# Fourier mixing and a squared-ReLU feed-forward layer on one core: a reordered prologue, half-width sine tables, weights staged in f32, and batch folds spaced out

## The chip, the cores and the metric

The kernel runs on one core of a Trainium2 chip. The metric is the device time of one execution in microseconds; a kernel is run several times and the median is quoted. The profiled span is a little shorter than the device time of the same execution (693.4 against 695.2 us for the kernel before). Engines are named as in the profile: PE (matmul), PEld (its weight loads), DVE (vector), ACT (scalar), POOL (which here issues most of the loads) and SP (which issues the stores). All runs in this text were in the fast state, and all of them gave correct results.

## The reference, cut to what matters

```python
def _attn_ref(x):                       # x: 8 x 3008 x 256, f32
    X = np.fft.fft(x, axis=1)
    X = np.fft.fft(X, axis=2)
    return X.real.astype(np.float32)

def _moe_ref(x, w_in, w_out):           # x: 24064 x 256, w_in: 256 x 2048, w_out: 2048 x 256
    h = np.maximum(x @ w_in, 0.0)
    return (h * h @ w_out).astype(np.float32)
```

## The kernel before: the parts that matter

The two transforms become matmuls with cosine and sine tables. Symmetry lets the kernel fold each batch first (sums and differences of mirrored rows and columns: `u`, `v`, `w` on DVE) and then multiply by tables a quarter as long. The transform over the 256 features is merged into w_in (`gmat` makes G1, G2 and G3). What is left per batch is a small block of table matmuls (`stage1_ops`, PSUM tile `pf`) in two blocks (even and odd frequencies), and then the long pipeline in steps of 256 columns and 256 hidden features.

```python
def gmat(c):                            # merged weights, 512 columns at a time
    ...                                 # 4 matmuls from cosD, sinD and win16
    act(G1[:, cs], pc, AF.Copy, bias=0.0, scale=1.0 / HS)
    act(G2[:, cs], ps, AF.Copy, bias=0.0, scale=-1.0 / HS)
    ts(out=G3[:, cs], in0=ps, scalar1=s3[:, 0:1], scalar2=None, op0=ALU.mult)

def fold_ops(b):                        # a list of 24 entries per batch: DVE operations and one load
    ...
    ops = [pair(q) for q in range(NQ)] + [pair0]      # x4 -> u, 6 x 0.68 us
    if b + 1 < B:
        ops.append(lambda: load_x(b + 1))             # x4 is free: start the next load
    ...                                               # u -> v -> w

alloc_pq(0)
fe, fo = fold_ops(0)
for f in table_ops(0) + fe: f()         # sine tables of block 0, then batch 0's fold
for c in range(F // 512): gmat(c)
for f in stage1_ops(0, 0, True): f()
...
spread(fo, 1, 5)                        # side work, laid into the steps
spread(table_ops(1), 4, 10)             # the tables of block 1
spread(stage1_ops(0, 1, True), 10, 16)
FOLD = {0: [1, 2, 3], 1: [4], 2: [5], 3: [6, 7]}      # during batch 0: fold 1, 2 and 3
...
for si, (c, fp) in enumerate(steps):    # 384 steps
    cur = x_front(c, fp)                # matmuls with G1, G2; first ReLU on ACT
    if prev is not None: x_back(prev)   # matmuls with G3; second ReLU; two squares on DVE
    ...                                 # 8 output matmuls (po) of an earlier chunk
    for f in side.get(si, []): f()
```

There is one buffer for x (`x4`), 24 KB on each partition. In the first eight steps there are no output matmuls, so PE has only 0.64 us of work a step there.

Of the kernel before, what the change touches and what calls it, by code (L numbers as in the profile page):

```python
# [9 lines left out]
F32 = mybir.dt.float32  # L10
F16 = mybir.dt.float16
I32 = mybir.dt.int32
AF = mybir.ActivationFunctionType
# [4 lines left out]
HS = 32.0  # L18
# [4 lines left out]
def kernel(  # L23
# [32 lines left out]
    bfp = ctx.enter_context(tc.tile_pool(name="bfp", bufs=4))  # L56
# [3 lines left out]
    tgp = ctx.enter_context(tc.tile_pool(name="tgp", bufs=2))  # L60
# [31 lines left out]
    zt = const.tile([4 * NQ, D], F32, name="zt")  # L92
    nc.vector.memset(zt, 0.0)
# [16 lines left out]
    def load_mid(b, eng):  # L110
        eng.dma_start(out=xm[:, 1 : NQ + 2 : NQ], in_=x[b : b + 1, 0 : M + 1 : M])
        eng.dma_start(out=xm[:, 3 : 3 * NQ + 3 : 3 * NQ - 1], in_=x[b : b + 1, QN : S : M])
# [13 lines left out]
    nc.scalar.dma_start(out=xm, in_=zt)  # L126
    load_mid(0, nc.scalar)
    win16 = const.tile([P, 2, F], F16, name="win16")
    for c in range(2):
        cs = slice(c * F // 2, (c + 1) * F // 2)  # L130
        nc.gpsimd.dma_start(out=win16[:, :, cs],
                            in_=moe_w_in[:, cs].rearrange("(c p) f -> p c f", p=P))
    wout16 = const.tile([P, NFC, D], F16, name="wout16")
    nc.gpsimd.dma_start(out=wout16, in_=moe_w_out.rearrange("(c p) o -> p c o", p=P))
# [4 lines left out]
    def vec(name, w=1):  # L139
        return const.tile([P, w], F32, name=name)  # L140
# [25 lines left out]
    ts(out=s3, in0=sgn, scalar1=2.0 / HS, scalar2=None, op0=ALU.mult)  # L166
# [10 lines left out]

    cosD = const.tile([P, 2, P], F16, name="cosD")
    sinD = const.tile([P, 2, P], F16, name="sinD")
    for c in range(2):  # L180
        dv = tgp.tile([P, 1], F32, name="dv", tag="dv")
        ts(out=dv, in0=pidx, scalar1=float(c * P), scalar2=None, op0=ALU.add)
        t = tgp.tile([P, P], F32, name="td", tag="td")
        ts(out=t, in0=jrow, scalar1=dv[:, 0:1], scalar2=1.0 / D, op0=ALU.mult, op1=ALU.mult)
        ts(out=t, in0=t, scalar1=R23, scalar2=None, op0=ALU.add)
        ts(out=t, in0=t, scalar1=R23, scalar2=-float(D), op0=ALU.subtract, op1=ALU.mult)
        m = tgp.tile([P, P], F32, name="md", tag="md")
        stt(out=m, in0=jrow, scalar=dv[:, 0:1], in1=t, op0=ALU.mult, op1=ALU.add)
        stt(out=t, in0=m, scalar=-1.0, in1=m, op0=ALU.mult, op1=ALU.max)
        act(sinD[:, c, 0 : P - 1], m[:, 0 : P - 1], AF.Sin, bias=0.0, scale=wD)  # L190
        act(cosD[:, c, 0 : P - 1], t[:, 0 : P - 1], AF.Sin, bias=hpi[:, 0:1], scale=-wD)  # L191
        nc.vector.memset(cosD[:, c, P - 1 : P], 1.0)
        nc.vector.tensor_copy(sinD[:, c, P - 1 : P], alt)
# [4 lines left out]

    def table_ops(blk):
        c0, n = BLK[blk]  # L200
        cs = slice(c0, c0 + n)

        def two(q0):
            qs = (q0, q0 + 1)
            t = {q: tgp.tile([P, HE], F32, name="tt", tag="tt")[:, 0:n] for q in qs}
            m = {q: tgp.tile([P, HE], F32, name="tm", tag="tm")[:, 0:n] for q in qs}
            for q in qs:
                ts(out=t[q], in0=krow[:, cs], scalar1=nfrac[:, q : q + 1], scalar2=R23,  # L208
                   op0=ALU.mult, op1=ALU.add)
            for q in qs:  # L210
                ts(out=t[q], in0=t[q], scalar1=R23, scalar2=-float(S),  # L211
                   op0=ALU.subtract, op1=ALU.mult)
            for q in qs:
                stt(out=m[q], in0=krow[:, cs], scalar=nval[:, q : q + 1], in1=t[q],  # L214
                    op0=ALU.mult, op1=ALU.add)
                act(sinT[:, q, cs], m[q], AF.Sin, bias=0.0, scale=tsc[:, q : q + 1])  # L216
            for q in qs:
                stt(out=t[q], in0=m[q], scalar=-1.0, in1=m[q], op0=ALU.mult, op1=ALU.max)
                act(cosT[:, q, cs], t[q], AF.Sin, bias=bcos[:, q : q + 1],  # L219
                    scale=tneg[:, q : q + 1])  # L220

        return [(lambda q=q: two(q)) for q in range(0, NQ, 2)]
# [3 lines left out]
    G3 = const.tile([P, F], F16, name="G3")  # L226

    def gmat(c):
        cs = slice(c * 512, (c + 1) * 512)
        pc = psx.tile([P, 512], F32, name="pc", tag="x")  # L230
        for t in range(2):
            mm(pc, cosD[:, t, :], win16[:, t, cs], t == 0, t == 1)
        ps = psx.tile([P, 512], F32, name="ps", tag="x")
        for t in range(2):
            mm(ps, sinD[:, t, :], win16[:, t, cs], t == 0, t == 1)
        act(G1[:, cs], pc, AF.Copy, bias=0.0, scale=1.0 / HS)
        act(G2[:, cs], ps, AF.Copy, bias=0.0, scale=-1.0 / HS)
        ts(out=G3[:, cs], in0=ps, scalar1=s3[:, 0:1], scalar2=None, op0=ALU.mult)

    eall = const.tile([P, 2, NQ, B], F16, name="eall")  # L240
    ez = const.tile([P, 2, NQ, P], F16, name="ez")
    nc.vector.memset(ez, 0.0)
    bf = {}
    PQ = {}
# [3 lines left out]
    def fold_ops(b):  # L248
# [22 lines left out]
        def edges(s):  # L271
            def f():
                nc.vector.tensor_copy(w[k, s, :, P - 1], v[k, s, :, 0])
                if b == 0:
                    nc.vector.tensor_copy(ez[k, s, :, P - 1], v[k, s, :, P])
                else:
                    nc.vector.tensor_copy(eall[k, s, :, b], v[k, s, :, P])
            return f
# [199 lines left out]
    for f in table_ops(0) + fe:  # L478
        f()
    for c in range(F // 512):  # L480
        gmat(c)
    for f in stage1_ops(0, 0, True):
        f()

# [4 lines left out]
    side = {}  # L489

    def spread(ops, lo, hi):
        for i, f in enumerate(ops):
            side.setdefault(lo + int((hi - lo) * i / len(ops)), []).append(f)

    spread(fo, 1, 5)
    spread(table_ops(1), 4, 10)
    spread(stage1_ops(0, 1, True), 10, 16)
    FOLD = {0: [1, 2, 3], 1: [4], 2: [5], 3: [6, 7]}
    EGRP = {0: [1, 2, 3], 3: [4, 5, 6, 7]}
    for b in range(B - 1):  # L500
        s0 = first_step[b]
        L = first_step[b + 1] - s0
        at = lambda z: s0 + int(z * (L - 1))
        f0_, f1_ = (0.3, 0.85) if b == 0 else (0.05, 0.75)
        nf = FOLD.get(b, [])
        for i, bb in enumerate(nf):
            w_ = (f1_ - f0_) / len(nf)
            spread(sum(fold_ops(bb), []), at(f0_ + w_ * i), at(f0_ + w_ * (i + 1)))
        side.setdefault(at(0.0) + 1, []).append(lambda bb=b + 1: alloc_pq(bb))
        spread(stage1_ops(b + 1, 0) + stage1_ops(b + 1, 1), at(0.55 if b == 0 else 0.05), at(0.85))  # L510
        if b in EGRP:
            spread(e_ops(EGRP[b]), at(0.87), at(0.97))
            side.setdefault(at(0.97), []).append(lambda bb=b + 1: e_row(bb))
        else:
            side.setdefault(at(0.3), []).append(lambda bb=b + 1: e_row(bb))
# [54 lines left out]
```

## Time and profile before

| | before |
|---|---|
| device time, median of the 4 runs beside the changed kernel | 695.44 us |
| PE busy | 92% of 693.4 us |
| PE busy from 0 to 140 us | 89.5 us |
| PE's longest waits | 26.6 us for ACT's ReLU, 17.9 us for w_in |

The first look is the page: the share of each of 40 slices (17.3 us each) in tenths.

```profile
PE   0748676999999999999999999999999999999998
PEclk9978988999999999999999999999999999999999
DMA  8920755518111631153101011111011111111111
```

PE is full from the eighth slice on, so nearly all that can be saved by feeding PE lies in the first 130 us. The table of stretches says it with numbers. Columns: the stretch, its length, busy us (and instructions) of PE, PEld, DVE, ACT, POOL, then the granted clock, the DMA engines' busy share and GB/s.

```profile
10.00:20.00 10.00, 2.12 (x6) 0.72 (x6) 8.96 (x21) 6.07 (x11) 3.72 (x4) 1.00 1.04 198
40.00:50.00 10.00, 2.97 (x14) 1.75 (x13) 8.22 (x24) 4.67 (x9) 0.00 (x0) 0.64 0.00 0
50.00:60.00 10.00, 5.92 (x34) 4.09 (x34) 6.66 (x18) 7.81 (x16) 0.00 (x0) 0.68 0.01 2
80.00:90.00 10.00, 2.31 (x21) 1.83 (x19) 2.40 (x5) 0.27 (x1) 1.84 (x3) 0.86 0.55 155
200.00:400.00 200.00, 200.00 (x1927) 175.12 (x1925) 126.82 (x342) 162.32 (x288) 17.11 (x20) 1.00 0.25 72
```

PE's list of waits, whole (us in total, times, longest):

```profile
PE xb L74 <- ACT r L460: 26.6, 6, 8.6
PE pc L74 <- DMA win_128<-in_moe_w_in_dram: 17.9, 1, 17.9
PE xb L74 <- DVE qt L338: 2.3, 2, 1.6
PE pc L74 <- DVE G_200 L238: 1.8, 1, 1.8
PE ps L74 <- ACT G_198 L236: 1.5, 2, 0.8
```

"Waiting for ACT's ReLU" doesn't yet say why the ReLU is late. The chain of waits around 80 us shows one of the causes: ACT waited for DVE, and DVE waited for x. Columns: start, us, what.

```profile
79.42 0.30 issue
79.73 7.85 DMA x_110<-in_x_dram,idx
87.60 0.21 DVE u L255
```

**A measure used all through this text.** I call the end of the second ReLU of a step the end of that step. Up to step 36, PE streams 63.99 us worth of matmul columns, counted in the trace at 2.4 GHz (all matmuls that start before the end of step 36, zeros left out). The number is the same in every kernel below. So the end of step 36 less 63.99 us is the time lost by then. The clock comes from the Trainium skill ("TensorE: Matmul & The Clock Gate", first table: up to 2.4 GHz). The trace agrees: matmuls of 256 columns start 0.11 us apart when nothing holds them. In the kernel before, step 36 ends at 131.31 us, so 67.3 us are lost.

### The profile page before, as it was taken

Reading aid. Unit: us, or ns where it says so; the run is one execution under the profiler, and the core shown is the slowest. Engines: PE = TensorE matmul, PEld = TensorE weight load, DVE = VectorE, ACT = ScalarE, POOL = GpSimd, SP = SyncE. Lnnn points to the kernel's source line nnn. Section 1 sums busy time; section 2 is a strip of 40 time slices with the busy share of each in tenths; the row PEclk is TensorE's granted clock in tenths of the full one; section 3 lists DMA queues with packets and bytes.
Section 4 is the critical chain, followed back from the end, with each engine's and each line's share of the span. In section 5 each row is a group of like instructions: output and inputs, shape, how many; then the busy total and the mean of one; then the engine's idle time right before and its main releaser. Section 6 shows DMA issues by size and latency. Waiting matters only on the chain.

```text
span 693.4 us, 14967 instructions
## 1 busy us (share of the span) xinstructions
PE 639.5 (92%) x5924; PEld 551.3 (80%) x5924; DVE 414.5 (60%) x1131; ACT 521.1 (75%) x936; POOL 79.6 (11%) x89
## 2 busy tenths in 40 slices
PE   0748676999999999999999999999999999999998
PEld 0326564788889888888878888898889888998886
DVE  8777487676656666488754555555554555545442
ACT  4467454778888888878878888878888878888883
POOL 6400653303000400040000000000000000000000
PEclk9978988999999999999999999999999999999999
DMA  8920755518111631153101011111011111111111
GB/s 215 215 51 20 206 150 132 155 45 204 49 39 47 166 92 46 47 151 107 47 31 48 31 46 42 37 47 48 31 47 47 32 46 41 46 38 46 48 46 48
DMA packets 37766, 52.56 MB, mean 76 GB/s; under 512 B 5136, under 2 KB 31304, under 8 KB 37696
## 3 DMA queue, kind: packets, MB, share of 16 engines
q0 software_dynamic: 9680, 25.36, 15.4%
q1 hardware_dynamic: 27972, 26.22, 11.9%
q8 instruction: 46, 0.75, 0.5%
q14 instruction: 24, 0.20, 0.1%
q10 hardware_dynamic: 44, 0.03, 0.0%
HBM read 29.00 MB, written 24.64 MB: 77 GB/s over the span
## 4 chain that ended last, share of the span: by engine, by line
PE 84%; DVE 6%; ACT 3%; POOL 2%; DMA 2%; issue 2%; DVEq 0%; ACTq 0%
PE po L74 46%; PE xb L74 34%; PE pf L74 5%; POOL x_110 L101 2%; DVE u L255 2%; DMA x_110<-in_x_dram,idx 1%; ACT sinT L216 1%; DMA x_110<-in_x_dram 1%; ACT cosT L219 1%; ACT r L460 1%; DVE tt L211 1%; DVE tm L214 1%; DVE tt L208 0%; ACT r L470 0%; DVE h_370 L474 0%
## 5 line engine op out<-in xcount | busy, mean ns | idle before, releaser
L460 ACT ACTIVATE r<-xb 128x512 f16<-128x512 f32 (+1 forms) x384 | 226.4, 590 | 114.9 <-PE xb L74 84.6
L470 ACT ACTIVATE r<-xb 128x512 f16<-128x512 f32 (+1 forms) x384 | 226.2, 589 | 21.7 <-PE xb L74 3.2
L74 PE MATMUL xb<-qt,G_199 128*128 128x256 f16 (+8 forms) x880 | 189.1, 258 | 2.3 <-DVE qt L338 2.3
L74 PE MATMUL xb<-pt,G_198 128*128 128x256 f16 (+8 forms) x880 | 189.8, 259 | 0.4
L74 PE MATMUL xb<-qt,G_200 128*128 128x256 f16 (+8 forms) x880 | 147.3, 259 | 26.6 <-ACT r L460 26.6
L74 PEld LDWEIGHTS <-G_200 128*128 128x128 f16 x880 | 82.0, 98 | 37.0 <-issue 27.7
L74 PEld LDWEIGHTS <-G_198 128*128 128x128 f16 x880 | 84.1, 98 | 16.3 <-issue 5.7
L74 PEld LDWEIGHTS <-G_199 128*128 128x128 f16 x880 | 81.1, 98 | 17.0 <-issue 1.7
L101 POOL DMA_INDIRECT x_110<-in_x_dram,idx x48 | 59.5, 1240 | 14.5 <-issue 14.3
L404 ACT ACTIVATE os<-po 128x512 f32<-128x512 f32 (+1 forms) x95 | 56.3, 592 | 5.0 <-PE po L74 4.0
L255 DVE TENSOR_TENSOR u<-x_110 127x510 f16<-127x510 f32 x48 | 31.0, 683 | 16.8 <-DMA x_110<-in_x_dram,idx 10.3
L116 POOL DMA_DIRECT2D x_110<-in_x_dram x14 | 7.9, 566 | 217.9 <-DVE u L259 217.9
L74 PE MATMUL pf<-cosT,w 127*128 127x377 f16 (+1 forms) x96 | 30.1, 341 | 0.0
L74 PE MATMUL pf<-sinT,w 127*127 127x377 f16 (+1 forms) x96 | 29.8, 335 | 0.0
L74 PEld LDWEIGHTS <-w 127*128 127x128 f16 (+1 forms) x192 | 23.3, 122 | 3.9 <-issue 1.4
L74 PE MATMUL pc<-win_128,cosD 128*128 128x512 f16 x8 | 4.1, 614 | 19.7 <-DMA win_128<-in_moe_w_in_dram 17.9
L267 DVE TENSOR_TENSOR w<-v 127x381 f16<-127x381 f16 x64 | 20.9, 354 | 0.0
L262 DVE TENSOR_TENSOR v<-u 127x512 f16<-127x512 f16 x48 | 18.9, 418 | 0.1
L74 PEld LDWEIGHTS <-cosD 128*128 128x128 f16 x8 | 1.0, 126 | 21.7 <-ACT cosD L191 9.2
L309 ACT ACTIVATE as<-pf 128x377 f32<-128x377 f32 (+7 forms) x34 | 16.6, 487 | 1.6 <-PE pf L74 1.4
L216 ACT ACTIVATE sinT<-tm,tsc 128x377 f16<-128x377 f32 (+1 forms) x12 | 6.8, 610 | 12.2 <-DVE tm L214 12.2
L74 PE MATMUL po<-wout_131,h_738 128*128 128x256 f16 x64 | 10.5, 291 | 0.0
(264 smaller groups left out, 1179.8 us busy)
## 6 DMA issues: line engine op xcount, KB each, us to landing
out_dram<-os SPq DMA_DIRECT2D x157, 128.0 KB
x_110<-in_x_dram POOLq DMA_DIRECT2D x14, 756.0 KB
x_110<-in_x_dram SPq DMA_DIRECT2D x6, 252.0 KB
win_128<-in_moe_w_in_dram POOLq DMA_DIRECT2D x2, 512.0 KB
wout_131<-in_moe_w_out_dram POOLq DMA_DIRECT2D x1, 1024.0 KB
x_110<-in_x_dram,idx POOLq DMA_INDIRECT x48
x_110<-in_x_dram POOLq DMA_DIRECT2D x14, 2.0 KB
out_dram<-os SPq DMA_DIRECT2D x2, 108.0 KB
```

What stands on the lines that cost most here:

```text
L74: nc.tensor.matmul(o, l, r, start=start, stop=stop, skip_group_check=True)
L101: nc.gpsimd.indirect_dma_start(out=x4[0:NP, 2 + s, 2 * part : 2 * part + 2, :].rearrange("p q d -> p (q d)"), out_offset=None, in_=bass.AP ...
L116: nc.gpsimd.dma_start(out=x4[0:NP, s, :, :], in_=up(b, s, 0, NQ))
L211: ts(out=t[q], in0=t[q], scalar1=R23, scalar2=-float(S), op0=ALU.subtract, op1=ALU.mult)
L216: act(sinT[:, q, cs], m[q], AF.Sin, bias=0.0, scale=tsc[:, q : q + 1])
L255: return lambda: vt(u[k, :, q, 1:D], x4[k, 0:2, q, 1:D], x4[k, 3:1:-1, NQ - 1 - q, D - 1 : 0 : -1], op=ALU.add)
L262: return lambda: vt(v[k, s, q : q + 2, :], u[k, 0, q : q + 2, :], u[k, 1, q : q + 2, :], op=ALU.subtract if s else ALU.add)
L267: return lambda: vt(w[k, i, q : q + 3, 0 : P - 1], v[k, s, q : q + 3, 1:P], v[k, s, q : q + 3, D - 1 : P : -1], op=ALU.add if i < 2 else A ...
L309: act(st["a"][0:m, :], st[0][0:m, :], AF.Copy, bias=0.0, scale=1.0) \
L404: act(os_[0:m], st["o"][0:m], AF.Copy, bias=0.0, scale=HS * HS)
L460: act(r[:, 0, :, 0:n], xb[:, :, 0:n], AF.Relu)
L470: act(r[:, 1, :, 0:n], xb[:, :, 0:n], AF.Relu)
```

## The change

Its intent is to start PE earlier and to keep it fed in the first 130 us.

- The sine tables are computed for half of their columns; the other half is the mirror image with a sign (twelve small copies per block, on ACT for block 0, on DVE for block 1).
- The weights come in as f32, into the buffers that later hold h, and ACT and DVE cast them. Before, the DMA cast them on the way.
- Ten matmuls on zeros run on PE while it has nothing to do.
- The tables come first, then the 128x128 matrices, then the fold. Only half of the merged weights are made before step 0.
- Only batch 1 is folded during batch 0; three batches follow in batch 1, well apart. Batch 1's "E" rows (the single middle feature column) are multiplied inline, as batch 0's were.

The diff, cut to its core:

```diff
-    nc.scalar.dma_start(out=xm, in_=zt)
-    load_mid(0, nc.scalar)
+    nc.sync.dma_start(out=xm, in_=zt)
+    load_mid(0, nc.sync)
...
-    for c in range(2):                       # cast in the DMA
-        nc.gpsimd.dma_start(out=win16[:, :, cs], in_=moe_w_in[...])
-    nc.gpsimd.dma_start(out=wout16, in_=moe_w_out...)
+    wst = h2p.tile([P, 2, F], F32, name="wst", tag="h2")
+    wot = h2p.tile([P, NFC, D], F32, name="wot", tag="h2")
+    for c in range(4):
+        nc.gpsimd.dma_start(out=wst[:, :, cs], in_=moe_w_in[...])
+    nc.gpsimd.dma_start(out=wot, in_=moe_w_out...)
...
+    def gcast(c, cp): cp(win16[:, :, cs], wst[:, :, cs])
+    def wcast(c): nc.vector.tensor_copy(wout16[:, cs, :], wot[:, cs, :])
...
     def table_ops(blk):
-        cs = slice(c0, c0 + n)
+        ng = (n + 1) // 2
+        cs = slice(c0, c0 + ng)              # Sin for these columns only
+        def mir(q, on_act): ...              # dst = d[:, q, c0 + n - 1 : ... : -1]
...
-    for f in table_ops(0) + fe: f()
-    for c in range(F // 512): gmat(c)
-    for f in stage1_ops(0, 0, True): f()
+    for i in range(NQ // 2): rd0[i](); tr0[2 * i](); tr0[2 * i + 1]()
+    nc.vector.memset(ez, 0.0)
+    dmats()
+    for f in mi0: f()
+    warm = psx.tile([P, 512], F32, name="warm", tag="x")
+    for _ in range(10):
+        mm(warm, cosD[:, 1, :], ez[:, 0, 0:4, :], True, True)
+    for f in fe: f()
+    gcast(0, nc.scalar.copy); gmat(0); rd1[0]()
+    ...                                      # stage1(0, 0), gcast(1), gmat(1), gcast(2), gcast(3)
...
-    spread(fo, 1, 5)
-    spread(table_ops(1), 4, 10)
-    spread(stage1_ops(0, 1, True), 10, 16)
-    FOLD = {0: [1, 2, 3], 1: [4], 2: [5], 3: [6, 7]}
+    spread([rd1[1], rd1[2]], 0, 2)
+    spread(tr1, 1, 4)
+    spread(fo, 2, 5)
+    spread(mi1, 5, 7)
+    spread([(lambda c=c: wcast(c)) for c in range(4)], 6, 9)
+    spread(stage1_ops(0, 1, True), 9, 13)
+    FOLD = {0: [(1, 0.35, 0.52)], 1: [(2, 0.02, 0.2), (3, 0.38, 0.56), (4, 0.7, 0.85)],
+            2: [(5, 0.1, 0.4)], 3: [(6, 0.1, 0.4)], 4: [(7, 0.1, 0.4)]}
```

More of the change, by code (lines that the diff above doesn't have):

```diff
@@ L55 @@
     uvp = ctx.enter_context(tc.tile_pool(name="uvp", bufs=1))
-    bfp = ctx.enter_context(tc.tile_pool(name="bfp", bufs=4))
+    bfp = ctx.enter_context(tc.tile_pool(name="bfp", bufs=3))
     pp = ctx.enter_context(tc.tile_pool(name="pp", bufs=2))
@@ L59 @@
     asp = ctx.enter_context(tc.tile_pool(name="asp", bufs=2))
-    tgp = ctx.enter_context(tc.tile_pool(name="tgp", bufs=2))
+    tgp = ctx.enter_context(tc.tile_pool(name="tgp", bufs=1))
     rp = ctx.enter_context(tc.tile_pool(name="rp", bufs=3))
@@ L92 @@
     zt = const.tile([4 * NQ, D], F32, name="zt")
+    ez = const.tile([P, 2, NQ, P], F16, name="ez")
     nc.vector.memset(zt, 0.0)
@@ L125 @@
             gather(0, 1 - s, NQ // 2 - 1 - part)
-    nc.scalar.dma_start(out=xm, in_=zt)
-    load_mid(0, nc.scalar)
+    nc.sync.dma_start(out=xm, in_=zt)
+    load_mid(0, nc.sync)
     win16 = const.tile([P, 2, F], F16, name="win16")
-    for c in range(2):
-        cs = slice(c * F // 2, (c + 1) * F // 2)
-        nc.gpsimd.dma_start(out=win16[:, :, cs],
-                            in_=moe_w_in[:, cs].rearrange("(c p) f -> p c f", p=P))
     wout16 = const.tile([P, NFC, D], F16, name="wout16")
-    nc.gpsimd.dma_start(out=wout16, in_=moe_w_out.rearrange("(c p) o -> p c o", p=P))
+    wst = h2p.tile([P, 2, F], F32, name="wst", tag="h2")
+    wot = h2p.tile([P, NFC, D], F32, name="wot", tag="h2")
+    for c in range(4):
+        cs = slice(c * F // 4, (c + 1) * F // 4)
+        nc.gpsimd.dma_start(out=wst[:, :, cs],
+                          in_=moe_w_in[:, cs].rearrange("(c p) f -> p c f", p=P))
+    nc.gpsimd.dma_start(out=wot, in_=moe_w_out.rearrange("(c p) o -> p c o", p=P))
     wS = 2.0 * math.pi / S
@@ L165 @@
     s3 = vec("s3")
-    ts(out=s3, in0=sgn, scalar1=2.0 / HS, scalar2=None, op0=ALU.mult)
+    ts(out=s3, in0=sgn, scalar1=-2.0, scalar2=None, op0=ALU.mult)
     ts(out=sgn, in0=sgn, scalar1=2.0, scalar2=-1.0, op0=ALU.mult, op1=ALU.add)
@@ L176 @@
     ts(out=alt, in0=alt, scalar1=4.0, scalar2=None, op0=ALU.mult)
+    nalt = vec("nalt")
+    ts(out=nalt, in0=alt, scalar1=-1.0, scalar2=None, op0=ALU.mult)
+    alt1 = vec("alt1")
+    stt(out=alt1, in0=top, scalar=2.0, in1=alt, op0=ALU.mult, op1=ALU.add)
+    nalt1 = vec("nalt1")
+    ts(out=nalt1, in0=alt1, scalar1=-1.0, scalar2=None, op0=ALU.mult)
+    MIR = [(nalt, nalt), (alt1, nalt1), (alt, alt), (nalt, alt), (nalt, nalt), (alt, nalt)]
     cosD = const.tile([P, 2, P], F16, name="cosD")
@@ L179, with dmats @@
     sinD = const.tile([P, 2, P], F16, name="sinD")
-    for c in range(2):
+    def dmats():
         dv = tgp.tile([P, 1], F32, name="dv", tag="dv")
-        ts(out=dv, in0=pidx, scalar1=float(c * P), scalar2=None, op0=ALU.add)
-        t = tgp.tile([P, P], F32, name="td", tag="td")
-        ts(out=t, in0=jrow, scalar1=dv[:, 0:1], scalar2=1.0 / D, op0=ALU.mult, op1=ALU.mult)
-        ts(out=t, in0=t, scalar1=R23, scalar2=None, op0=ALU.add)
-        ts(out=t, in0=t, scalar1=R23, scalar2=-float(D), op0=ALU.subtract, op1=ALU.mult)
-        m = tgp.tile([P, P], F32, name="md", tag="md")
-        stt(out=m, in0=jrow, scalar=dv[:, 0:1], in1=t, op0=ALU.mult, op1=ALU.add)
-        stt(out=t, in0=m, scalar=-1.0, in1=m, op0=ALU.mult, op1=ALU.max)
-        act(sinD[:, c, 0 : P - 1], m[:, 0 : P - 1], AF.Sin, bias=0.0, scale=wD)
-        act(cosD[:, c, 0 : P - 1], t[:, 0 : P - 1], AF.Sin, bias=hpi[:, 0:1], scale=-wD)
-        nc.vector.memset(cosD[:, c, P - 1 : P], 1.0)
-        nc.vector.tensor_copy(sinD[:, c, P - 1 : P], alt)
+        ts(out=dv, in0=pidx, scalar1=float(P), scalar2=None, op0=ALU.add)
+        dvs = (pidx, dv)
+        t = [tgp.tile([P, P], F32, name="td", tag=f"td{_}") for _ in range(2)]
+        m = [tgp.tile([P, P], F32, name="md", tag=f"md{_}") for _ in range(2)]
+        for c in range(2):
+            ts(out=t[c], in0=jrow, scalar1=dvs[c][:, 0:1], scalar2=1.0 / D,
+               op0=ALU.mult, op1=ALU.mult)
+        for c in range(2):
+            ts(out=t[c], in0=t[c], scalar1=R23, scalar2=None, op0=ALU.add)
+        for c in range(2):
+            ts(out=t[c], in0=t[c], scalar1=R23, scalar2=-float(D), op0=ALU.subtract, op1=ALU.mult)
+        for c in range(2):
+            stt(out=m[c], in0=jrow, scalar=dvs[c][:, 0:1], in1=t[c], op0=ALU.mult, op1=ALU.add)
+        for c in range(2):
+            stt(out=t[c], in0=m[c], scalar=-1.0, in1=m[c], op0=ALU.mult, op1=ALU.max)
+            nc.vector.memset(cosD[:, c, P - 1 : P], 1.0)
+            nc.vector.tensor_copy(sinD[:, c, P - 1 : P], alt)
+            act(sinD[:, c, 0 : P - 1], m[c][:, 0 : P - 1], AF.Sin, bias=0.0, scale=wD)
+            act(cosD[:, c, 0 : P - 1], t[c][:, 0 : P - 1], AF.Sin, bias=hpi[:, 0:1], scale=-wD)
@@ L197, with red @@
     BLK = ((0, HE), (HE, HO))
+    HG = HE // 2 + 1
     def table_ops(blk):
         c0, n = BLK[blk]
-        cs = slice(c0, c0 + n)
-        def two(q0):
+        ng = (n + 1) // 2
+        cs = slice(c0, c0 + ng)
+        tb = {}
+        def red(q0):
+            if q0 == 0:
+                tb["t"] = tgp.tile([P, NQ, HG], F32, name="tt", tag="tt")
+                tb["m"] = tgp.tile([P, NQ, HG], F32, name="tm", tag="tm")
             qs = (q0, q0 + 1)
-            t = {q: tgp.tile([P, HE], F32, name="tt", tag="tt")[:, 0:n] for q in qs}
-            m = {q: tgp.tile([P, HE], F32, name="tm", tag="tm")[:, 0:n] for q in qs}
+            t, m = tb["t"][:, :, 0:ng], tb["m"][:, :, 0:ng]
@@ L207, in two @@
             for q in qs:
-                ts(out=t[q], in0=krow[:, cs], scalar1=nfrac[:, q : q + 1], scalar2=R23,
+                ts(out=t[:, q], in0=krow[:, cs], scalar1=nfrac[:, q : q + 1], scalar2=R23,
                    op0=ALU.mult, op1=ALU.add)
             for q in qs:
-                ts(out=t[q], in0=t[q], scalar1=R23, scalar2=-float(S),
+                ts(out=t[:, q], in0=t[:, q], scalar1=R23, scalar2=-float(S),
                    op0=ALU.subtract, op1=ALU.mult)
             for q in qs:
-                stt(out=m[q], in0=krow[:, cs], scalar=nval[:, q : q + 1], in1=t[q],
+                stt(out=m[:, q], in0=krow[:, cs], scalar=nval[:, q : q + 1], in1=t[:, q],
@@ L215, in two @@
                     op0=ALU.mult, op1=ALU.add)
-                act(sinT[:, q, cs], m[q], AF.Sin, bias=0.0, scale=tsc[:, q : q + 1])
             for q in qs:
-                stt(out=t[q], in0=m[q], scalar=-1.0, in1=m[q], op0=ALU.mult, op1=ALU.max)
-                act(cosT[:, q, cs], t[q], AF.Sin, bias=bcos[:, q : q + 1],
-                    scale=tneg[:, q : q + 1])
-        return [(lambda q=q: two(q)) for q in range(0, NQ, 2)]
+                stt(out=t[:, q], in0=m[:, q], scalar=-1.0, in1=m[:, q], op0=ALU.mult, op1=ALU.max)
@@ new lines, in trig, with mir @@
+        def trig(q):
+            act(sinT[:, q, cs], tb["m"][:, q, 0:ng], AF.Sin, bias=0.0, scale=tsc[:, q : q + 1])
+            act(cosT[:, q, cs], tb["t"][:, q, 0:ng], AF.Sin, bias=bcos[:, q : q + 1],
+                scale=tneg[:, q : q + 1])
+        def mir(q, on_act):
+            nm = n // 2
+            src = slice(c0, c0 + nm)
+            a, b = (cosT, sinT) if q % 2 else (sinT, cosT)
+            for d, sr, sc in ((cosT, a, MIR[q][0]), (sinT, b, MIR[q][1])):
+                dst = d[:, q, c0 + n - 1 : c0 + n - 1 - nm : -1]
+                if on_act:
+                    act(dst, sr[:, q, src], AF.Copy, bias=0.0, scale=sc[:, 0:1])
+                else:
+                    ts(out=dst, in0=sr[:, q, src], scalar1=sc[:, 0:1], scalar2=None, op0=ALU.mult)
@@ L224 @@
+        return ([(lambda q=q: red(q)) for q in range(0, NQ, 2)],
+                [(lambda q=q: trig(q)) for q in range(NQ)],
+                [(lambda q=q: mir(q, blk == 0)) for q in range(NQ)])
     G1 = const.tile([P, F], F16, name="G1")
@@ L226, with gcast @@
     G3 = const.tile([P, F], F16, name="G3")
+    def gcast(c, cp):
+        cs = slice(c * 512, (c + 1) * 512)
+        cp(win16[:, :, cs], wst[:, :, cs])
     def gmat(c):
@@ L237, in gmat, with gneg @@
         act(G2[:, cs], ps, AF.Copy, bias=0.0, scale=-1.0 / HS)
-        ts(out=G3[:, cs], in0=ps, scalar1=s3[:, 0:1], scalar2=None, op0=ALU.mult)
+    def gneg(c):
+        cs = slice(c * 512, (c + 1) * 512)
+        ts(out=G3[:, cs], in0=G2[:, cs], scalar1=s3[:, 0:1], scalar2=None, op0=ALU.mult)
     eall = const.tile([P, 2, NQ, B], F16, name="eall")
-    ez = const.tile([P, 2, NQ, P], F16, name="ez")
-    nc.vector.memset(ez, 0.0)
     bf = {}
+    INL = (0, 1)
     PQ = {}
@@ L273, in f @@
                 nc.vector.tensor_copy(w[k, s, :, P - 1], v[k, s, :, 0])
-                if b == 0:
+                if b in INL:
                     nc.vector.tensor_copy(ez[k, s, :, P - 1], v[k, s, :, P])
@@ L477 @@
     fe, fo = fold_ops(0)
-    for f in table_ops(0) + fe:
-        f()
-    for c in range(F // 512):
-        gmat(c)
-    for f in stage1_ops(0, 0, True):
-        f()
+    rd0, tr0, mi0 = table_ops(0)
+    rd1, tr1, mi1 = table_ops(1)
+    for i in range(NQ // 2):
+        rd0[i]()
+        tr0[2 * i]()
+        tr0[2 * i + 1]()
+    nc.vector.memset(ez, 0.0)
+    dmats()
+    for f in mi0:
+        f()
+    warm = psx.tile([P, 512], F32, name="warm", tag="x")
+    for _ in range(10):
+        mm(warm, cosD[:, 1, :], ez[:, 0, 0:4, :], True, True)
+    for f in fe:
+        f()
+    gcast(0, nc.scalar.copy)
+    gmat(0)
+    rd1[0]()
+    s1 = stage1_ops(0, 0, True)
+    for f in s1[0:NQ]:
+        f()
+    gcast(1, nc.vector.tensor_copy)
+    for f in s1[NQ:]:
+        f()
+    gneg(0)
+    gmat(1)
+    gneg(1)
+    for c in (2, 3):
+        gcast(c, nc.vector.tensor_copy)
     steps = [(c, fp) for c in range(len(chunks)) for fp in range(NF)]
@@ L489 @@
     side = {}
+    pre = {}
     def spread(ops, lo, hi):
@@ L493, in spread, with wcast @@
             side.setdefault(lo + int((hi - lo) * i / len(ops)), []).append(f)
-    spread(fo, 1, 5)
-    spread(table_ops(1), 4, 10)
-    spread(stage1_ops(0, 1, True), 10, 16)
-    FOLD = {0: [1, 2, 3], 1: [4], 2: [5], 3: [6, 7]}
-    EGRP = {0: [1, 2, 3], 3: [4, 5, 6, 7]}
+    for c in range(2, F // 512):
+        side.setdefault(2 * c - 4, []).extend([lambda c=c: gmat(c), lambda c=c: gneg(c)])
+    def wcast(c):
+        cs = slice(c * NFC // 4, (c + 1) * NFC // 4)
+        nc.vector.tensor_copy(wout16[:, cs, :], wot[:, cs, :])
+    spread([rd1[1], rd1[2]], 0, 2)
[6 more added lines that the diff above has]
+            2: [(5, 0.1, 0.4)], 3: [(6, 0.1, 0.4)], 4: [(7, 0.1, 0.4)]}
+    ST1 = {0: (0.55, 0.95), 1: (0.25, 0.85)}
+    EGRP = {1: [2, 3, 4], 4: [5, 6, 7]}
     for b in range(B - 1):
@@ L503 @@
         at = lambda z: s0 + int(z * (L - 1))
-        f0_, f1_ = (0.3, 0.85) if b == 0 else (0.05, 0.75)
-        nf = FOLD.get(b, [])
-        for i, bb in enumerate(nf):
-            w_ = (f1_ - f0_) / len(nf)
-            spread(sum(fold_ops(bb), []), at(f0_ + w_ * i), at(f0_ + w_ * (i + 1)))
+        for bb, lo, hi in FOLD.get(b, []):
+            spread(sum(fold_ops(bb), []), at(lo), at(hi))
         side.setdefault(at(0.0) + 1, []).append(lambda bb=b + 1: alloc_pq(bb))
-        spread(stage1_ops(b + 1, 0) + stage1_ops(b + 1, 1), at(0.55 if b == 0 else 0.05), at(0.85))
+        lo, hi = ST1.get(b, (0.05, 0.85))
+        spread(stage1_ops(b + 1, 0, b + 1 in INL) + stage1_ops(b + 1, 1, b + 1 in INL), at(lo), at(hi))
         if b in EGRP:
-            spread(e_ops(EGRP[b]), at(0.87), at(0.97))
+            spread(e_ops(EGRP[b]), at(0.87), at(0.96))
             side.setdefault(at(0.97), []).append(lambda bb=b + 1: e_row(bb))
-        else:
+        elif b + 1 not in INL:
             side.setdefault(at(0.3), []).append(lambda bb=b + 1: e_row(bb))
```

## The prediction

> What bounds the kernel now. From about 130 us to the end TensorE decides: the table of stretches has it busy 200.00 of 200 us in both long stretches, and it waits for nothing after 140 us. The cost is in the start. From 0 to 140 us PE is busy only about 89.5 us; its list of waits names 26.6 us on ACT (r, first ReLU), the longest 8.6 us, and 17.9 us on the DMA of w_in. Counting matmul columns at 2.4 GHz against the end of each ReLU step, some 65 us of the first 131 us (37 steps) are lost: 28.6 before step 0 ends at 36.6 us; about 16 in steps 4 to 9; 2 at step 15; 10 at steps 20-21; 9 at steps 28-30. Later steps lose about 0.045 us each.
>
> Who causes it. In the timeline DVE starts the batch fold (u) only at 19.9 us, though x has landed by about 14 us: the sine tables come first. At 41 to 58 us the second table block's reductions and Sin calls (0.61 and 0.69 us each) sit in order before the ReLUs. The chain of waits shows the folds of batches 2 and 3 waiting for x loads started only when the fold before freed the single x buffer: 7.9 and 5.5 us of DMA, loads of 20 and 16 us. While PE idles its granted clock falls to 0.64-0.68 (40-60 us). The Trainium skill ("TensorE: Matmul & The Clock Gate", "Why this matters for your kernels") says a few us of idleness return the clock to half; these stretches agree.
>
> The change, costed (estimates from these durations).
> 1. Half-width tables: a pair of reductions costs DVE about 1.9 instead of 3.1 us; tables, zeroing and D matrices end at about 13 us, the fold at 20 instead of 26. Twelve mirrors on ACT (2.6 to 4 us) end at 16-18 us.
> 2. f32 weights: twice the bytes landed, 4.2 MB at about 215 GB/s: w_in quarters at 17 to 25 us, w_out at 34, x of batch 1 at 48-50 instead of 39.5. The first cast on ACT, 1 us; seven on DVE, 0.6 to 1.1 us each. Batch 1 is folded at step 13 (about 50 us): tight, not late.
> 3. Ten zero matmuls fill idle PE time and keep the clock; worth 1 us at most.
> 4. Step 0 ends at about 26.5 us (-10). Steps 0 to 9 are then DVE-bound (about 18 us): step 9 at 46 instead of 60.3.
> 5. Spaced folds: loads finish before their folds; the stops at steps 15, 20-21, 28-30 (21 us) nearly vanish. Three dense folds in batch 1 may stop PE 0.5 to 1 us each.
> 6. Added PE work: batch 1's E rows inline, 12 matmuls of 377 columns, 1.9 us.
>
> Sum: 10 + 4 + 21, less 1.9 and about 2 of new stops: about 32 us, all on the critical path, as PE is saturated behind it; steady part and tail stay. Predicted 662 us, range 654 to 670. Faster by over 2%: 0.97; within 2%: 0.025; slower: 0.005.
>
> What would show it: u starts at 13-14 us; step 0's second ReLU ends at 25-28; step 9 at 44-48; no PE wait over 2 us after 50; DMA busy unbroken until about 48; PE busy share about 96%.
>
> What would make it wrong: DVE standing in order at a cast whose quarter lands late, pushing step 0 to 30 us; w_out's cast delaying the first output matmuls; batch 1's x late at step 13; batch 4's fold (step 72) meeting an unfinished load.

## The result, and the profile after

The changed kernel takes 663.78 us (median of 4, 663.04 to 664.68) against 695.44 us; the ratio is 0.9546, with a 95% interval from 0.9525 to 0.9567. Ratios in this text are the mean time of one kernel's fast runs over that of the other's fast runs of the same rounds, so not quite the ratio of the medians. Two more sets of the changed kernel gave 664.90 us (ratio 0.9563) and 663.63 us (0.9560).

The slices and the stretches after:

```profile
PE   1679999999999999999999999999999999999997
PEclk9989999999999999999999999999999999999999
DMA  7963614584528111541111111111111111111111
```

```profile
10.00:20.00 10.00, 5.46 (x17) 2.12 (x18) 9.53 (x35) 8.21 (x22) 8.21 (x10) 1.00 0.77 234
20.00:30.00 10.00, 7.37 (x43) 4.07 (x42) 8.44 (x25) 6.00 (x13) 5.27 (x5) 1.00 1.04 313
30.00:40.00 10.00, 5.23 (x30) 3.33 (x30) 8.58 (x32) 9.68 (x22) 3.17 (x3) 0.90 1.01 204
40.00:50.00 10.00, 9.11 (x70) 6.96 (x69) 9.62 (x29) 6.45 (x13) 0.00 (x0) 0.93 0.30 69
80.00:90.00 10.00, 10.00 (x88) 8.46 (x87) 5.78 (x15) 7.76 (x14) 0.00 (x0) 1.00 0.18 54
```

PE is full from 50 us on, where before it was full only from 130 us on. Its waits are now small, except the first one:

```profile
PE warm L74 <- ACT cosD L212: 13.7, 1, 13.7
PE xb L74 <- ACT r L507: 2.9, 2, 1.4
PE pc L74 <- DVE win_129 L271: 2.0, 2, 1.3
PE ps L74 <- ACT r L517: 1.9, 1, 1.9
PE po L74 <- DVE wout_130 L571: 0.9, 1, 0.9
```

The ends of steps, from the traces of one profiled execution each (us; the runs below are in the table as well):

| kernel | step 0 | step 9 | step 19 | step 20 | step 27 | step 28 | step 36 | lost by then | step 383 |
|---|---|---|---|---|---|---|---|---|---|
| before | 36.57 | 60.26 | 79.78 | 91.34 | 104.57 | 114.48 | 131.31 | 67.3 | 685.65 |
| changed | 29.14 | 46.87 | 65.28 | 66.83 | 79.21 | 81.06 | 96.19 | 32.2 | 653.49 |
| folds alone | 35.72 | 59.40 | 80.67 | 82.49 | 95.48 | 97.34 | 112.47 | 48.5 | 670.05 |
| prologue alone | 29.04 | 47.20 | 65.17 | 78.27 | 92.33 | 101.39 | 119.09 | 55.1 | 673.47 |
| before, two x buffers | 35.70 | 59.39 | 80.57 | 82.10 | 95.06 | 98.32 | 113.63 | 49.6 | 670.91 |
| changed, full tables | 34.82 | 53.77 | 72.03 | 73.58 | 85.96 | 87.82 | 102.94 | 39.0 | 660.20 |
| changed, cast in the DMA | 27.60 | 45.27 | 63.53 | 65.07 | 77.46 | 79.31 | 94.44 | 30.4 | 652.02 |
| that, late tables, fold at 16 | 26.88 | 42.31 | 60.91 | 62.86 | 75.67 | 77.52 | 92.65 | 28.7 | 650.19 |

Of the 35.1 us won by step 36, 7.4 come before step 0 ends, 6.0 between steps 0 and 9 (17.7 instead of 23.7 us), and 21.7 between steps 9 and 36 (49.3 instead of 71.1 us). After step 36, 3.0 us are given back; of these, 1.9 us are PE work that the change adds (606.1 us of columns in all against 604.2).

### The profile page after: what moved, and what is told of

It reads as the page before. It is cut to its first block, busy times and chain, and to the rows that moved or that the text cites. A ratio compares the mean times of both kernels' runs of the same rounds, so it can differ in the third digit from the quotient of the medians.

```text
span 661.3 us, 15041 instructions
## 1 busy us (share of the span) xinstructions
PE 634.9 (96%) x5946; PEld 549.9 (83%) x5946; DVE 408.8 (62%) x1152; ACT 523.3 (79%) x949; POOL 91.5 (14%) x91
## 4 chain that ended last, share of the span: by engine, by line
PE 93%; DVE 2%; ACT 2%; POOL 1%; issue 1%; DMA 1%; POOLq 0%
PE po L74 50%; PE xb L74 37%; PE pf L74 6%; POOL x_110 L102 1%; DMA x_110<-in_x_dram,idx 1%; ACT sinT L246 0%; ACT cosT L247 0%; ACT r L507 0%; ACT r L517 0%; DVE u L302 0%; DVE w L314 0%; PE pc L74 0%; DVE win_129 L271 0%; ACT G_183 L281 0%; DVE v L309 0%
## 5 line engine op out<-in xcount | busy, mean ns | idle before, releaser
L74 PEld LDWEIGHTS <-G_184 128*128 128x128 f16 x880 | 80.8, 97 | 17.1 <-issue 1.3
L102 POOL DMA_INDIRECT x_110<-in_x_dram,idx x48 | 69.7, 1452 | 20.3 <-issue 13.4
L74 PE MATMUL warm<-ez,cosD 128*128 128x512 f16 x10 | 4.2, 601 | 13.7 <-ACT cosD L212 13.7
L356 ACT ACTIVATE as<-pf 128x377 f32<-128x377 f32 (+5 forms) x32 | 15.5, 486 | 0.9 <-PE pf L74 0.8
L74 PE MATMUL po<-wout_130,h_387 128*128 128x256 f16 x64 | 9.6, 272 | 0.9 <-DVE wout_130 L571 0.9
L74 PE MATMUL po<-wout_130,h_761 128*128 128x256 f16 x64 | 9.6, 273 | 0.0
```

The source lines that it names most:

```text
L74: nc.tensor.matmul(o, l, r, start=start, stop=stop, skip_group_check=True)
L102: nc.gpsimd.indirect_dma_start(out=x4[0:NP, 2 + s, 2 * part : 2 * part + 2, :].rearrange("p q d -> p (q d)"), out_offset=None, in_=bass.AP ...
L356: act(st["a"][0:m, :], st[0][0:m, :], AF.Copy, bias=0.0, scale=1.0) \
```

## The experiments

Eleven runs: eight edited kernels, one of them twice, and the changed kernel itself twice as a yardstick. They are told by subject, not in the order in which they ran.

### The two halves of the change, each alone

The kernel before with only the new fold schedule:

```diff
 # in the kernel before
-    FOLD = {0: [1, 2, 3], 1: [4], 2: [5], 3: [6, 7]}
-    EGRP = {0: [1, 2, 3], 3: [4, 5, 6, 7]}
+    FOLD = {0: [(1, 0.35, 0.52)], 1: [(2, 0.02, 0.2), (3, 0.38, 0.56), (4, 0.7, 0.85)], ...}
+    ST1 = {0: (0.55, 0.95), 1: (0.25, 0.85)}
+    EGRP = {1: [2, 3, 4], 4: [5, 6, 7]}      # and INL = (0, 1)
```

> The kernel before, with only the new schedule of folds, second-stage blocks and E rows (batch 1's E rows inline). Theory: its stops at steps 15, 20-21 and 28-30 (about 21 us) came of the time that an x load takes into the one buffer, so they vanish although each fold is as dense as before (24 operations in 7 to 9 steps); the added inline E rows cost 1.9 us: 675 to 679 us. Rival: the stops come of the density of fold work on DVE; then they stay, moved to batch 1, and the time is 690 us or more.

Measured: 678.16 us (ratio 0.9746, interval 0.9721 to 0.9771). Steps 20 and 28 end 1.8 and 1.9 us after steps 19 and 27, where before it took 11.6 and 9.9 us. A fold still has its 24 entries in 7 to 9 steps, so the density of the folds was not what stopped PE there. (The profile is of the slowest of the four runs, 679.63 us; the fastest took 675.95 us.)

The changed kernel with the old fold schedule is the counterpart (`FOLD`, `ST1`, `EGRP` and `INL` put back, `bfp` with 4 buffers).

> The changed kernel with the schedule of folds, blocks and E rows of before (bfp again 4). Theory: the prologue alone brings 12 to 15 us and the stops of about 19 us come back around steps 20 and 28: 680 to 684 us, and the two parts add up (this gain plus that of the run with the new folds alone is the whole within 2 us). Rival: the parts depend on one another, because the earlier start lets the x loads collide with the weights or with one another; then the sum misses by over 4 us.

Measured: 683.34 us (0.9837, 0.9815 to 0.9858). The stops are back. PE's list of waits of this run begins:

```profile
PE xb L74 <- ACT r L507: 18.4, 4, 10.6
PE warm L74 <- ACT cosD L212: 14.0, 1, 14.0
```

and its chain of waits shows what lies behind the ReLU:

```profile
67.17 0.82 POOL x L102
67.98 0.18 issue
68.16 6.36 DMA x<-in_x_dram
74.52 0.01 issue
74.53 0.10 DVE u L302
```

The two gains in medians of the same rounds are 17.1 and 11.9 us, together 29.0, where the whole change brought 31.7. So they don't quite add up: I had expected a miss within 2 us or over 4 us, and it is 2.7 us (4.1 us at step 36 in the traces). The table shows where. With the early prologue and the old folds, step 20 takes 13.1 us instead of 11.6: the load takes nearly as long as before (18.8 us from issue to the fold's first use, against 19.7), but PE gets to the fold sooner (step 19 ends 9.5 us after the load's issue instead of 11.8), so it waits longer. An earlier start is thus partly eaten by the load time unless the folds are moved too. By the times alone the 2.7 us are not clear of the noise, as the runs of the folds alone spread over 3.7 us; the longer stop is what the traces show. In the run with the folds alone, a stop of 1.9 us at step 15 and one of 1.2 us at step 10 remain, which the whole change doesn't have.

### One load, one buffer: the cause of the large stops

If the stops are the time of a load into the only x buffer, a second buffer must remove them without touching the schedule:

```diff
 # in the kernel before
-    x4 = xp.tile([P, 4, NQ, D], F32, name="x4")
+    x4s = [xp.tile([P, 4, NQ, D], F32, name=f"x4{i}", tag=f"x4{i}") for i in range(2)]
...
-        if b + 1 < B:
-            ops.append(lambda: load_x(b + 1))
+        if b + 2 < B:                        # load_x(1) is issued after the weights
+            ops.append(lambda: load_x(b + 2))
...
-    osp = ctx.enter_context(tc.tile_pool(name="osp", bufs=4))
+    osp = ctx.enter_context(tc.tile_pool(name="osp", bufs=2))
```

> The kernel before with its own prologue and its own schedule of folds, but with two buffers for x, so that the load of batch b+2 starts when batch b has been folded (the output staging shrinks from 4 to 2 buffers to make room). If the stops at steps 20-21 and 28-30 are the time of a load into the one buffer, they vanish with no change of the schedule: 695 less 17 to 19 us, 675 to 680 us. If the density of the folds on DVE were the cause, the stops stay: 690 to 697 us. A slip of under 2 us from the smaller output staging would show as ACT waiting for a DMA of os.

Measured: 681.29 us (0.9806, 0.9786 to 0.9825), 13.5 us less than before, so somewhat less than I had expected; the stop at step 20 is gone (1.5 us), and that at step 28 as well (3.3 us, of which 3.1 are matmul columns). Its list of waits has kept the waits of the first steps and gained one:

```profile
PE xb L74 <- ACT r L463: 13.0, 5, 5.8
PE xb L74 <- DMA qt<-es: 1.3, 1, 1.3
```

At step 36 it stands at 113.6 us, 17.7 us ahead of before, as much as I had expected of the stops; 3 us of that are lost later, 1.4 of them at step 39, where PE waits for the E row of batch 1, which the faster steps reach before its copy has landed. Spacing the folds and a second buffer cure the same stop, each in its own way. Since this run left the folds as dense and where they were, that settles the cause. In the trace of before, the loads of batches 2 and 3 were issued at 67.9 and 93.1 us, when the fold in front had freed the buffer, and the last data that the fold needed came at 87.6 and 109.1 us, 19.7 and 16.0 us later; DVE had stood ready for them since 77.3 and 102.7 us.

### Half-width tables, or only the order?

```diff
 # in the changed kernel
-        ng = (n + 1) // 2
+        ng = n                               # Sin for every column; no mirrors
...
-    for f in mi0: f()
-    spread(mi1, 5, 7)
```

> The changed kernel with both table blocks computed at full width (Sin for every column, no mirrors), the order of operations kept. Theory: the halving is worth what DVE saves in front of the first fold, 3 x 1.2 us, and as much again less 2.4 us of mirrors in steps 1 to 7: step 0 ends at about 31 to 33 us instead of 29.1, and the time is 667 to 670 us. Rival: the twelve mirrors on ACT and twelve on DVE cost what the halving saves, and the order alone did it: 663 to 665 us. Rival 2: x lands at about 15 us, so DVE does the fold's first part no earlier anyway, and the loss is only 1 to 2 us.

Measured: 669.80 us (0.9634, 0.9617 to 0.9650), 4.9 us more than the changed kernel in the same rounds (664.90). So the halving is worth about 5 us. What it does first is seen where DVE starts the fold, in the kernel before and in the changed one:

```profile
19.89 3.68 DVE L255 TENSOR_TENSOR u<-x_110 127x510 f16<-127x510 f32 x6
```

```profile
12.98 2.48 DVE L302 TENSOR_TENSOR u<-x_110 127x510 f16<-127x510 f32 x4
```

With full tables the fold starts at 16.91 us. Step 0 ends at 34.8 us, later than I had expected. The timeline shows how: the zeros start 3.9 us later (17.62 against 13.69 us), because DVE's reductions are longer,

```profile
17.62 4.45 PE L74 MATMUL warm<-ez,cosD 128*128 128x512 f16 x10 [17.62 <-ACT cosD L212]
28.18 0.60 PE L74 MATMUL pc<-win,cosD 128*128 128x512 f16 x2 [2.12 <-DVE win L271]
```

and the second weight product then waits 2.1 us for a cast on DVE, which stands behind the first full-width reduction of block 1. The same reduction at half width cost less in the changed kernel: its second product waited 0.71 us. The mirrors don't eat the gain.

What the rest of the prologue is worth can be read only as a difference: full tables against the folds alone, 669.80 against 678.16 us (0.9634 against 0.9746 of before), some 8 us for the new order, the weights made in halves, the f32 staging and the zeros together. The last two have runs of their own below (about 3 us lost, about 1 us won). The new order, which would then be the largest part of the prologue's gain, was not run alone.

Nor would a still earlier start of the fold bring much, because it has come up against the landing of x. In the profile of the changed kernel's second set DVE waited for x twice within the first fold:

```profile
14.91 1.29 DVE L302 TENSOR_TENSOR u<-x 127x510 f16<-127x510 f32 x2 [0.98 <-DMA x<-in_x_dram]
16.61 1.89 DVE L302 TENSOR_TENSOR u<-x 127x510 f16<-127x510 f32 x3 [0.40 <-DMA x<-in_x_dram]
```

Its u was done at 18.62 us and its step 0 ended at 30.59 us. In the profiles of the first and third sets u was done at 17.16 and 17.05 us, and step 0 ended at 29.14 us in both. So the landing of x alone moves the changed kernel by 1.5 us from one execution to the next, and effects of that size must be read with it in mind.

### The zeros

```diff
 # in the changed kernel
-    warm = psx.tile([P, 512], F32, name="warm", tag="x")
-    for _ in range(10):
-        mm(warm, cosD[:, 1, :], ez[:, 0, 0:4, :], True, True)
```

> The changed kernel without its ten matmuls on zeros. Theory of the prediction: worth 1 us at most, so 663.8 to 664.8 us. Rival: the zeros matter more, because without them the first weight products and the first DFT block (18 matmuls of 377 columns, 0.16 us each at full clock) run at half clock from about 18.7 us on; the timeline of the changed kernel leaves only about 1 us of slack between the last of them and DVE's qt at 23.2 us, so step 0 would end 2 to 3 us later: 666 to 667 us. The granted clock between 10 and 30 us and the duration of the pf matmuls tell them apart.

Measured: 665.17 us (0.9575, 0.9556 to 0.9594). This is 1.4 us over the first set of the changed kernel, and 0.3 us over the second, so it was run again beside the changed kernel.

> The same kernel as in the first run without zeros, now in the same rounds as the changed kernel, since 665.2 against 663.8 and 664.9 us does not settle it. Prediction's theory: 0 to 1 us slower than the changed kernel beside it. Rival: 2 to 3 us slower. In the first look the two first products and the first six pf matmuls took 4.6 us instead of 1.8 us, and step 0 ended 1.3 us later than in one profile of the changed kernel and 0.2 us earlier than in the other.

(The 4.6 us in this expectation were misread: in the first run's trace it is 3.47 us from the first product to the seventh pf matmul.)

> The changed kernel, unaltered, as the yardstick in the same rounds: 663.5 to 665 us.

Measured: 665.01 us (0.9584, 0.9553 to 0.9614) against 663.63 us (0.9560, 0.9533 to 0.9588). The means of all sets are 665.4 us (10 runs) and 664.2 us (14 runs). The difference of these means is 1.2 us, with a standard error of 0.4; the sets overlap, so no more than "about 1 us" can be said from the times. The trace says where it can come from. Without zeros (second run; start, us):

```profile
19.01 1.01 PE L74 MATMUL pc<-win,cosD 128*128 128x512 f16 x2 [19.01 <-ACT win L271]
19.82 1.06 PE L74 MATMUL ps<-win,sinD 128*128 128x512 f16 x2
20.67 1.66 PE L74 MATMUL pf<-cosT,w 127*128 127x377 f16 x6
22.17 0.64 PE L74 MATMUL pf<-cosT,ez 127*128 127x377 f16 x3
```

With zeros:

```profile
18.73 0.59 PE L74 MATMUL pc<-win_129,cosD 128*128 128x512 f16 x2 [0.85 <-ACT win_129 L271]
19.16 0.59 PE L74 MATMUL ps<-win_129,sinD 128*128 128x512 f16 x2
19.59 1.13 PE L74 MATMUL pf<-cosT,w 127*128 127x377 f16 x6
20.55 0.65 PE L74 MATMUL pf<-cosT,ez 127*128 127x377 f16 x3
```

From the first product to the start of the last line it takes 3.16 us without and 1.82 us with zeros, and neither run waits in between. How much of these 1.3 us reaches step 0 depends on x. Without zeros, u was done at 17.59 and 18.90 us in the two profiles, and step 0 ended at 30.43 and 30.85 us; with zeros, 17.16 us went with 29.14 and 18.62 us with 30.59. Moved along with the fold, the kernel with zeros would stand at about 29.6 and 30.9 us, so the zeros win about 0.9 us where x comes early and nothing where it comes late (an estimate from these four profiles). The Trainium skill ("TensorE: Matmul & The Clock Gate", "The HAM clock gate") says that an idle PE runs at half its clock, and returns to full clock after some 3.4 us of work. The traces agree on the half clock: a pair of products of 512 columns starts 0.81 us after the pair before it cold (19.01 to 19.82) and 0.43 us warm. On the time they agree roughly: the clock record goes to full 3.4 and 2.8 us after the first product without zeros, and 3.8, 5.0 and 5.3 us after the first zero in the three profiles of the changed kernel, in all three within 0.3 us of the first product or before it.

### The weights: cast by the DMA again

```diff
 # in the changed kernel
-    wst, wot, gcast(...), wcast(...)         # f32 staging and all eight casts
+    for c in range(2):
+        nc.gpsimd.dma_start(out=win16[:, :, cs], in_=moe_w_in[...])
+    nc.gpsimd.dma_start(out=wout16, in_=moe_w_out...)
```

> The changed kernel with the weights cast on the way in by the DMA again, as before did (w_in in two halves), so without the eight casts on ACT and DVE. If staging in f32 is what makes the weights come early, this is slower: 665 to 668 us. My theory: staging is no gain here, because before's first half of w_in landed at 17.9 us with the cast in the DMA, against 17.65 us plus 1.0 us of ACT cast in the changed kernel, and the casts of the third and fourth quarter stand on DVE in front of the third weight product (PE waits 1.3 us for it at 26.1 us), those of w_out before the first output matmuls: 2 to 4 us faster, 660 to 662 us.

Measured: 661.58 us (0.9512, 0.9488 to 0.9536). Against the means of the changed kernel's three sets (664.2 us) this is 3.0 us less (mean 661.2). The rival, that f32 staging brings the weights in sooner, falls: the first product starts at 18.16 us, right behind the zeros, instead of at 18.73 us, and PE's waits for casts are gone:

```profile
18.16 0.59 PE L74 MATMUL pc<-win,cosD 128*128 128x512 f16 x2
```

The changed kernel's casts stood in order on DVE like this:

```profile
25.11 0.35 DVE L286 TENSOR_SCALAR G_185<-G_184,s_161 128x512 f16<-128x512 f16 x1 [0.28 <-ACT G_184 L282]
25.38 1.30 DVE L271 CAST win_129<-wst 128x1024 f16<-128x1024 f32 x2
```

```profile
26.13 0.60 PE L74 MATMUL pc<-win_129,cosD 128*128 128x512 f16 x2 [1.30 <-DVE win_129 L271]
```

The cast of the third quarter came only after qt and the G3 of the first two quarters, for the second of which DVE waited on ACT; and PE held the rest of step 0 behind the third product. In the run with the cast in the DMA this product starts at 24.55 us. In the profiles all of the gain is there when step 0 ends (27.6 us, against 29.1, 30.6 and 29.1 us), although x came 1.0 us late for the fold in this run; from there to step 383 this kernel and the changed one both take 624.4 us. By these profiles it is the casts before the end of step 0 that cost; the four of w_out, in steps 6 to 9, cost nothing that shows. The DMA itself loses nothing: from 18 to 27 us it landed 362 GB/s of f32 in the changed kernel (first line), and 224 GB/s here (second line), of mostly f16, half the bytes per weight.

```profile
18.00:27.00 9.00, 6.26 (x34) 3.38 (x34) 8.30 (x24) 4.52 (x9) 6.67 (x7) 1.00 1.01 362
```

```profile
18.00:27.00 9.00, 7.69 (x45) 4.40 (x44) 8.00 (x27) 5.32 (x11) 6.76 (x7) 1.00 1.31 224
```

### A better kernel

Steps 1 to 3 of the changed kernel take 2.5, 3.8 and 2.5 us; ACT runs almost without a gap there, with the twelve Sin calls of block 1 and the copies of the last weight product among the ReLUs (9.68 of 10 us in the stretch above), and DVE is 86% busy. So I moved block 1's tables back:

```diff
 # in the kernel with the cast in the DMA
-    rd1[0]()                                 # before stage1(0, 0)
-    spread([rd1[1], rd1[2]], 0, 2)
-    spread(tr1, 1, 4); spread(fo, 2, 5); spread(mi1, 5, 7)
-    spread(stage1_ops(0, 1, True), 9, 13)
+    for i, si in enumerate((1, 3, 5)):
+        side.setdefault(si, []).append(rd1[i])
+    spread(tr1, 4, 10); spread(fo, 5, 10); spread(mi1, 8, 11)
+    spread(stage1_ops(0, 1, True), 11, 16)
```

> A try at a better kernel: the weights cast in the DMA as in the run of that name, and the second table block moved back: its reductions to steps 1, 3, 5, its Sin calls to steps 4 to 9, mirrors to 8 to 10, the second DFT block of batch 0 to 11 to 15. In steps 1 to 3 of the changed kernel ACT and DVE are both busy over 85 per cent and PE loses 2 us a step; later steps have spare time. Theory: 1 to 3 us less than that run (661.6), so 658.5 to 660.5 us, and about 4 us less than the changed kernel. Rival: work moved only meets the same limit later, as ACT is full in all of the first eight steps: 661 to 662 us.

> The changed kernel itself, unaltered, as the yardstick for the runs beside it: 663 to 665 us.

Measured: 662.15 us (0.9539, 0.9511 to 0.9567; one run of five at 666.64), against 664.90 us of the changed kernel beside it. Not better than the run with the cast in the DMA alone (661.58): the rival was right about the sum, though not for its reason. Step 9 ended 2.1 us earlier (43.19 against 45.27 us), but at step 15 a stop of 1.7 us came: the second block's qt now stood on DVE behind the u operations of batch 1's fold, and step 16 needs it. In the list of waits it is

```profile
PE xb L74 <- DVE qt L379: 1.5, 1, 1.5
```

The kernel before had the same stop at its step 15 (1.8 us). So the fold has to start later:

```diff
-    spread(stage1_ops(0, 1, True), 11, 16)
-    FOLD = {0: [(1, 0.35, 0.52)], ...
+    spread(stage1_ops(0, 1, True), 11, 15)
+    FOLD = {0: [(1, 0.42, 0.58)], ...
```

> The run with late tables lost 1.7 us at step 15 (its DVE had the qt of batch 0's second block behind the first u operations of batch 1's fold, as the kernel before had at its step 15). Here that fold starts at step 16 instead of 13 and the block ends one step earlier. Theory: that stop goes and nothing else changes: 1.7 us less than that run, about 660.4 us. Rival: the stop moves to where the fold now stands, 662 us.

Measured: 659.39 us (659.14 to 659.81; 0.9494, 0.9468 to 0.9520), against 663.63 us (0.9560) of the changed kernel in the same rounds. It is the fastest of all, 0.7% below the changed kernel. The run before it was 2.8 us faster than the changed kernel beside it and this one is 4.2 us faster, so the later fold brought about 1.5 us, near the 1.7 us expected; the two were not run in the same rounds. The wait for qt is gone, and no wait of PE after the first is over 0.7 us at a time.

## Why the prediction was right, and where its terms were off

The predicted time, 662 us (654 to 670), held: 663.78 us. The sum of the predicted terms was 10 + 4 + 21 - 1.9 - 2 = 31 to 32 us; the profiled spans differ by 32.1 us. But the terms were not all as good as their sum, and two of them missed in opposite directions (points 5 and 6).

1. *What bounds it, and that all gain lies on the critical path*: right. Up to step 36 each kernel has the same 63.99 us of columns, and 35.1 us less are lost; after it only 3.0 us come back.
2. *Half-width tables*: right on DVE: u starts at 12.98 us (predicted 13 to 14). The run with full tables shows that this part alone is worth about 5 us.
3. *f32 weights, "4.2 MB at about 215 GB/s"*: wrong in the rate. 215 GB/s is what the x loads reach; the weights moved at 362 GB/s from 18 to 27 us. The x of batch 1 had therefore landed by about 45 us, not 48 to 50: the DMA share is 0.34 from 42 to 45 us and 0.00 after it. It did no harm, since the fold at step 13 came after both.
4. *"Ten zero matmuls ... worth 1 us at most"*: not contradicted; 1.2 us by the times, with a standard error of 0.4, and in the profiles 1.3 us of PE work, of which none to 0.9 us reach the end of step 0.
5. *"Step 0 ends at about 26.5 us (-10)"*: the term that was most off. Three profiles of the changed kernel have 29.1, 30.6 and 29.1 us (the 30.6 with a late x), so the gain was 6 to 7.4 us. My list of dangers had the cause, "DVE standing in order at a cast", but not quite the reason: the quarter was not late (the last of the four was issued at 14.7 us and took 8.9 us to land; the third was cast from 25.38 us on), the cast stood behind other work of DVE, the G3 of the quarter before last of all. With the casts taken out, step 0 ends at 27.6 us.
6. *"Steps 0 to 9 are then DVE-bound (about 18 us)"*: the time was right (17.7 us), the engine only half so. From 30 to 40 us ACT is busy for 9.68 of 10 us and PE waits for its ReLUs; from 40 to 50 us it is DVE with 9.62. That ACT alone held steps 1 to 3 wasn't tested by itself: the run with late tables moved work of both engines. The prediction was also not at one with itself here: 18 us after a step 0 at 26.5 us make 44.5 us, not the 46 that it gave for step 9, and its sum counted 4 us for this stretch, where 6.0 us were won. So two misses, 2.6 us too much at step 0 and 2 us too little after it, cancelled out. The mechanisms were right, but that the sum came within 1 us was luck in part.
7. *Spaced folds, 21 us*: right in size and cause: 21.7 us between steps 9 and 36, and both the schedule alone and a second buffer alone remove the large stops. I had credited the fold schedule with the 2 us at step 15; that stop stays with the folds alone (1.9 us) and is gone with the new prologue, which finishes the second block earlier. It is a matter of DVE's order.
8. *Dense folds in batch 1, "about 2 us of new stops"*: hardly there. Between steps 36 and 88 no step group of eight loses more than 0.7 us, save the one with the E rows (1.0 us).
9. *Batch 1's E rows, 1.9 us of PE*: right (606.1 against 604.2 us of columns).

## What to carry to other kernels

Where one engine is full in the long run, look only at the stretch before it gets there, and count there what it has to do against the time that it takes; each lost microsecond has a step, and a step has an engine that stood in order behind something. A wait for an activation can be a wait for a load two engines away, as here; with one buffer, the distance between two uses must be longer than the load, or a second buffer is needed, and an earlier start of everything else can make that wait longer (13.1 against 11.6 us at step 20). Before comparing two runs that differ by 1 or 2 us, look whether their inputs landed at the same time. Before casting on an engine to spare the DMA, see whether the DMA needs sparing: here the casts cost about 3 us on engines whose work stood in order behind other work, and the DMA lost nothing by casting.

## What the Trainium skill lacked or had wrong

- "TensorE: Matmul & The Clock Gate" warns that the recorded clock events can't be fully trusted. It doesn't say what this case shows: the clock record of a trace can begin only when the clock first goes to full (32.6 us in the kernel before, 22.4 and 21.8 us in the runs without zeros), and the clock column of the profile reads 1.00 for the time before that, though the first products ran at half clock there (0.81 us for two of 512 columns). Later idle stretches do show (0.64 from 40 to 50 us). At a start, read the durations, not the column.
- "DMA: Bandwidth & Descriptors" ("SWDGE vs HWDGE vs iDMA") says that a cast during a transfer must be issued from GpSimd, but gives no rate for it. Here the stretch with the cast weights landed 224 GB/s, mostly f16, the one with f32 weights 362 GB/s: as many weights per microsecond or more (224/2 against 362/4, though the first stretch holds a little of the next x load).
- The same page ("Bandwidth") has 341 GB/s for 1 MB issued from GpSimd. The f32 weights, in 128 partitions and pieces of 0.5 and 2 MB, are in line with it at 362 GB/s. The x loads, in 126 partitions, half of them gathers, reach about 200 GB/s (206 GB/s at a DMA share of 1.00 from 36 to 42 us of the changed kernel; a share of 1.00 is no ceiling, as the run with the cast in the DMA has 1.31). The page has no figure for that; why they are slower was not tested.
